# Four weight blocks split in three steps, an early half clock in the plan, and a new order table

## The chip, the cores and the metric

The kernel runs on one core of a Trainium2 chip, which has five engines that run side by side and wait for each other with semaphores: PE (matrix products), DVE and ACT (vector work), POOL (GpSimd, vector work in SBUF alone) and SP, which issues transfers. The metric is the device time of one execution in microseconds, less is better; the time before is the median of three runs.

## The reference

An attention that is causal by blocks of 64, and after it a feed-forward network with a gate made by a convolution along the sequence.

```python
scores = scale * np.matmul(q, k.transpose(0, 1, 3, 2))     # q, k, v: 8 batches, 8 heads, 576 x 64
mask = block_i >= block_j                                  # block = position // 64
attn = softmax(np.where(mask, scores, -1e9))
x = (attn @ v)                                             # heads side by side: 8 x 576 x 512
h = np.maximum(x @ w_in, 0.0)                              # w_in 512 x 1024
for k in range(3):
    conv_out += conv_w[k][None, None, :] * hp[:, k:k + S, :]
gate = 1.0 / (1.0 + np.exp(-conv_out))
return (h * gate @ w_out).astype(np.float32)               # w_out 1024 x 512
```

## The kernel before

The inputs are float32. A product that must keep float32 accuracy is made of float16 halves: an operand is split into a high half (the rounded value) and a low half (what the rounding left), and three products (high-high, low-high, high-low) are added up in PSUM. Splitting is work of the vector engines, the products are PE's.

The work goes through 8 batches. Batch 0 goes in two parts of the sequence, A (the first 256 positions) and B (the rest), with products in float32 and transposes on PE; batches 1 to 7 go whole, pair of heads by pair of heads (four pairs a batch): `stage_s` makes the scores (L1108), their maxima (L1207, DVE), the exponentials (L1210, ACT) and two float16 planes of the probabilities (L1057 to L1079, any of three engines); a DMA transposes the planes (L1097); `pair_pv` multiplies them with v (L1491) and its result is split into x (L1496, L1499, L1502). After four pairs `ffn` multiplies x with w_in (L1544), makes the gate (L1566 to L1592), splits it (L1596, L1599 the cast, L1603 the difference) and multiplies with w_out (L1637); the result is scaled (L1647, L1650) and stored.

The weights arrive once, as 16 blocks (8 of w_in, 8 of w_out) of 128 x 512 numbers. `load_w` and `decode` unpack each (L882 on ACT, L885 on POOL, L889, L892, L897 on DVE; a block's largest value L920 to L926), `scale_w` finds one scale for each matrix, and `split_w` makes the halves: `fh` multiplies a block by the scale and rounds (L951 on ACT, L954 on POOL), `fl` multiplies once more and takes the high half off (L960, DVE, `wih`/`wil` of w_in, `woh`/`wol` of w_out). The first output product (L1637) needs the halves of all eight blocks of w_out.

Order and engines come from a planner (`Plan`). Each piece of work is an operation with an engine, a planned duration and dependencies, and some can go to another engine (`other`). The table `TARGETS` has a number for each operation: a quarter of it is its place in its engine's queue, the remainder says which of the engines it takes. `Plan.order` plays the queues through with the planned durations, PE's clock among them (`speed`: full or half), and so fixes the order in which all engines get their instructions. Where it sees PE idle for over 0.4 us it puts in filling matmuls (`work`, L1774, a product of a constant with itself into a free bank), as many as fit before the next matmul by its plan.

Two operations at the very start matter here: `rounded_identity` (L643, DVE) writes `rident`, which the score products with the mask (L1337) and the transposes on PE (L1407) use; `blank` (L664) is a tile of zeros, on which the first group of fills runs. `stage_sa` makes the scores of part A (L1333, L1337), a group of eight matmuls for each pair of heads; their maxima are L1351.

## Time and profile before

| | us |
|---|---|
| median of three runs | 619.45 |
| lowest, highest | 618.64, 619.97 |
| profiled execution, its own time | 621.78 |
| its span, first to last instruction | 619.9 |
| PE, DVE, ACT, POOL busy in it | 597.5, 530.7, 481.6, 386.9 |

The profile is of one execution, whose own time is 1.88 us above its span. PE's busy time holds the filling matmuls as well. A group of matmuls is pipelined, so that the time of a group is its first start to its last end, and less than the sum of its members. The chain of waits is followed back from the last instruction: what stands on it had nothing between it and the end.

### The profile page before, as it was taken

Reading aid. Unit: us, or ns where it says so; the run is one execution under the profiler, and the core shown is the slowest. Engines: PE = TensorE matmul, PEld = TensorE weight load, DVE = VectorE, ACT = ScalarE, POOL = GpSimd, SP = SyncE. Lnnn points to the kernel's source line nnn. Section 1 sums busy time; section 2 is a strip of 40 time slices with the busy share of each in tenths; the row PEclk is TensorE's granted clock in tenths of the full one; section 3 lists DMA queues with packets and bytes.
Section 4 is the critical chain, followed back from the end, with each engine's and each line's share of the span. In section 5 each row is a group of like instructions: output and inputs, shape, how many; then the busy total and the mean of one; then the engine's idle time right before and its main releaser. Section 6 shows DMA issues by size and latency. Waiting matters only on the chain.

```text
span 619.9 us, 15505 instructions
## 1 busy us (share of the span) xinstructions
PE 597.5 (96%) x5832; PEld 381.2 (61%) x5832; DVE 530.7 (86%) x1122; ACT 481.6 (78%) x1234; POOL 386.9 (62%) x496
## 2 busy tenths in 40 slices
PE   8998899979999999999999999999999999999997
PEld 5556454447765477655775567555765667566754
DVE  5999999999889988999999998889889966973850
ACT  5999997796798659997799767978888857962721
POOL 4876665664495846986597454787786617852440
PEclk9999999999999999999999999999999999999999
DMA  8584412799938997699997699459886880594002
GB/s 296 206 293 146 139 35 92 170 224 192 255 78 217 195 221 129 139 196 218 198 189 139 143 223 227 110 116 209 188 172 117 195 145 18 108 163 120 1 1 86
DMA packets 205503, 97.77 MB, mean 158 GB/s; under 512 B 185308, under 2 KB 187636, under 8 KB 205428
## 3 DMA queue, kind: packets, MB, share of 16 engines
q1 hardware_dynamic: 203556, 93.63, 67.1%
q10 hardware_dynamic: 1872, 3.15, 1.8%
q8 instruction: 46, 0.75, 0.5%
q14 instruction: 29, 0.24, 0.1%
HBM read 41.44 MB, written 9.44 MB: 82 GB/s over the span
## 4 chain that ended last, share of the span: by engine, by line
PE 62%; DVE 25%; ACT 6%; POOL 3%; issue 2%; DMA 2%; DVEq 0%; ACTq 0%; POOLq 0%
PE banks L1637 22%; PE banks L1544 21%; PE banks L1491 8%; PE banks L1108 8%; DVE su L1207 3%; DVE t L1573 2%; PE banks L1774 2%; DVE ptbm L1063 2%; DVE t L1592 1%; DVE shared L897 1%; DVE ptbl L1063 1%; DVE st L1288 1%; DVE shared L892 1%; DVE vb L831 1%; DVE h L1063 1%
## 5 line engine op out<-in xcount | busy, mean ns | idle before, releaser
L1637 PE MATMUL banks<-woh,shared 128*128 128x512 f16 (+1 forms) x592 | 184.8, 374 | 0.3 <-DVE t L1592 0.3
L1544 PE MATMUL banks<-x,wih 128*128 128x288 f16 (+2 forms) x1024 | 156.7, 286 | 2.0 <-DVE t L1592 1.8
L1637 PEld LDWEIGHTS <-shared 128*128 128x128 f16 x888 | 82.7, 98 | 100.7 <-issue 15.0
L1544 PEld LDWEIGHTS <-wih 128*128 128x128 f16 x1024 | 98.0, 98 | 36.5 <-issue 8.6
L1207 DVE TENSOR_REDUCE su<-banks 128x1 f32<-128x192 f32 (+8 forms) x252 | 110.8, 478 | 3.1 <-PE banks L1108 2.2
L1637 PE MATMUL banks<-wol,shared 128*128 128x512 f16 (+1 forms) x296 | 110.5, 373 | 0.0
L1586 POOL TENSOR_TENSOR t<-t,shared 128x575 f32<-128x575 f32 x51 | 74.8, 1468 | 54.1 <-DVE t L1573 46.7
L1603 POOL TENSOR_TENSOR shared<-t,shared 128x576 f16<-128x576 f32 (+2 forms) x59 | 71.8, 1219 | 26.0 <-DVE shared L1599 12.8
L1544 PE MATMUL banks<-x,wil 128*128 128x288 f16 (+2 forms) x512 | 86.3, 286 | 0.6 <-DVE wil L960 0.6
L1108 PE MATMUL banks<-k,q 64*64 64x192 f32 (+9 forms) x1120 | 82.7, 414 | 3.9 <-DVE t L1592 1.1
L1491 PEld LDWEIGHTS <-vb 128*64 128x64 f16 x1848 | 63.0, 113 | 11.6 <-issue 10.9
L1573 DVE SCALAR_TENSOR_TENSOR t<-banks,cwb,t 128x575 f32<-128x575 f32 (+2 forms) x72 | 53.0, 742 | 12.5 <-ACT t L1569 7.5
L1108 PEld LDWEIGHTS banks<-k,q 64*64 64x64 f32 x1120 | 42.5, 132 | 33.9 <-issue 12.1
L1589 ACT ACTIVATE t<-t 128x576 f32<-128x576 f32 (+2 forms) x72 | 45.1, 629 | 23.1 <-POOL t L1586 16.5
L1544 PEld LDWEIGHTS <-wil 128*128 128x128 f16 x512 | 49.3, 98 | 14.9 <-DVE wil L960 1.2
L1592 DVE SCALAR_TENSOR_TENSOR t<-t,banks 128x576 f32<-128x576 f32 (+2 forms) x72 | 48.7, 680 | 8.4 <-ACT t L1589 7.6
L1569 ACT ACTIVATE t<-banks,cwb 128x576 f32<-128x576 f32 (+2 forms) x72 | 49.0, 684 | 6.6 <-DVE banks L1566 5.2
L1563 ACT ACTIVATE banks<-banks 128x576 f32<-128x576 f32 (+2 forms) x53 | 30.2, 574 | 15.8 <-PE banks L1544 15.4
L1210 ACT ACTIVATE p3f<-banks,su 128x512 f32<-128x512 f32 (+1 forms) x56 | 36.7, 659 | 5.5 <-DVE su L1207 2.2
L1582 ACT ACTIVATE shared<-banks,cwb 128x575 f32<-128x575 f32 x51 | 37.6, 738 | 1.9 <-DVE t L1573 0.8
L1647 ACT ACTIVATE stage<-banks,osc 128x512 f32<-128x512 f32 (+1 forms) x29 | 19.3, 668 | 24.7 <-PE banks L1637 24.7
L1210 ACT ACTIVATE p2f<-banks,su 128x384 f32<-128x384 f32 (+1 forms) x56 | 30.8, 552 | 8.3 <-DVE su L1207 4.4
(206 smaller groups left out, 1186.9 us busy)
## 6 DMA issues: line engine op xcount, KB each, us to landing
k<-in_k_dram SPq DMA_DIRECT2D x28, 368.0 KB, 3.7
vn<-in_v_dram SPq DMA_DIRECT2D x32, 320.0 KB, 3.9
q<-in_q_dram SPq DMA_DIRECT2D x28, 320.0 KB, 3.7
out_dram<-stage SPq DMA_DIRECT2D x24, 256.0 KB, 2.9
shared<-in_moe_w_in_dram SPq DMA_DIRECT2D x8, 512.0 KB, 4.1
shared<-in_moe_w_out_dram SPq DMA_DIRECT2D x8, 512.0 KB, 3.7
out_dram<-stage ACTq DMA_DIRECT2D x11, 256.0 KB, 3.7
k<-in_k_dram SPq DMA_DIRECT2D x4, 240.0 KB, 4.8
```

Source lines behind the costliest of these rows:

```text
L1108: nc.tensor.matmul(out[64 * y:64 * y + 64], t["q"].ap[64 * r:64 * r + 64, q0:q0 + 64], t["k"].ap[64 * r:64 * r + 64, k0:k0 + c1 - c0], sta ...
L1207: nc.vector.tensor_reduce(out=st.ap[:, k:k + 1], in_=home[hh].ap[:, x], op=ALU.max, axis=AX.X, negate=True)
L1210: nc.scalar.activation(out=y.ap[:, 0:n], in_=home[hh].ap[:, x], func=AF.Exp, bias=st.ap[:, k:k + 1], accum_out=st.ap[:, 9 + k:10 + k])
L1491: nc.tensor.matmul(y, vb.ap[:, w, c, j, :], x, start=first, stop=(z == 1 and c == jobs[-1][0]), skip_group_check=True)
L1544: nc.tensor.matmul(h(a, z), wt[:, c, fs], xs[c][xi].ap[:, x0 + a:x0 + z], start=(n + c - c0 == 0), stop=(n + c - c0 == 3 * NCC - 1))
L1569: nc.scalar.activation(out=t.ap[:, 0:no], in_=h(own, own + no), func=AF.Copy, scale=cwb.ap[:, NFC + f:NFC + f + 1])
L1573: nc.vector.scalar_tensor_tensor(out=t.ap[:, i0:no], in0=h(own + i0 - 1, own + no - 1), scalar=cwb.ap[:, f:f + 1], in1=t.ap[:, i0:no], op0 ...
L1586: nc.gpsimd.tensor_tensor(out=t.ap[:, 0:i1], in0=t.ap[:, 0:i1], in1=u.ap[:, 0:i1], op=ALU.add)
L1589: nc.scalar.activation(out=t.ap[:, 0:no], in_=t.ap[:, 0:no], func=AF.Tanh)
L1592: nc.vector.scalar_tensor_tensor(out=t.ap[:, 0:no], in0=t.ap[:, 0:no], scalar=1.0, in1=h(own, own + no), op0=ALU.add, op1=ALU.mult)
L1603: eng.tensor_tensor(out=g[1][:, f, carry:carry + no], in0=t.ap[:, 0:no], in1=g[0][:, f, carry:carry + no], op=ALU.subtract)
L1637: nc.tensor.matmul(fb.ap[:, 0:cut], g[a][:, f, cs], w[:, f, ds], start=(f == 0 and n == 0), stop=(f == NFC - 1 and n == 2))
```

## The change

It has four parts. Four of the eight blocks of w_out (9, 11, 13 and 15, `WPL`) are split in three steps: the block is multiplied by the scale in place (`sc`), copied and rounded into the high half (`h`), and the low half is the plain difference (`low`). Each step is planned on POOL and can go to another engine. The plan takes PE's clock as half until 8.5 us (`COLD`), PE as free from 1.9 us, and 0.95 us for each of the first three groups of scores. All fills use `rident`. The table has new numbers throughout.

```diff
 TARGETS = """
-0 0 4 8 16 0 4 24 28 12 16 44 64 52 129 80 196 92 185 88 181 252 140 104 280 288 448 8 12 9 4 12 16 8 40 13 32 36 20 64 44 52 44 56 96 40 200 60 60 88
+0 0 12 8 4 0 4 28 40 16 24 20 76 52 169 88 224 108 185 84 181 276 144 112 296 304 388 8 16 17 8 12 20 12 44 4 32 36 12 32 20 32 24 28 48 44 196 40 129
...
+    COLD = 8.5
+
     def order(self, targets, fill, clock):
...
-            return 1.0 if full else 2.0
+            return 1.0 if full and t > self.COLD else 2.0
...
-        free = [1.1, 0.0, 0.0, 0.0, 0.75]
+        free = [1.9, 0.0, 0.0, 0.0, 0.75]
...
+    WPL = (9, 11, 13, 15)
...
-    made = [pl.op(DVE, 2.45, rounded_identity, -80.0)]
+    made = [pl.op(DVE, 1.9, rounded_identity, -80.0)]
...
+        def sc(eng=nc.gpsimd):
+            eng.tensor_scalar(out=g.ap, in0=g.ap, scalar1=s_(), scalar2=0.0, op0=ALU.mult, op1=ALU.add)
+
+        def sc_a():
+            nc.scalar.activation(out=g.ap, in_=g.ap, func=AF.Copy, scale=s_())
+
+        def h(eng=nc.gpsimd):
+            eng.tensor_scalar(out=hi, in0=src(), scalar1=1.0, scalar2=0.0, op0=ALU.mult, op1=ALU.add)
+
+        def h_a():
+            nc.scalar.activation(out=hi, in_=src(), func=AF.Copy)
+
+        def low(eng=nc.gpsimd):
+            eng.tensor_tensor(out=lo, in0=src(), in1=hi, op=ALU.subtract)
+
+        if f in WPL:
+            o = pl.op(POOL, c_pool(512) + 0.08, sc, at, deps=[o, d], bufs=[g, fac, wm],
+                      other=((ACT, c_act(512, False, True), sc_a), (DVE, c_dve(512, True) + 0.07, partial(sc, nc.vector), True)))
+            o = pl.op(POOL, c_pool(512), h, at, deps=[o], bufs=[g],
+                      other=((ACT, c_act(512, False), h_a), (DVE, c_dve(512, True), partial(h, nc.vector), True)))
+            wdone[f] = pl.op(POOL, c_pool(512, True), low, at + 0.7, deps=[o], bufs=[g],
+                             other=((DVE, c_dve(512) + 0.01, partial(low, nc.vector), True),))
+            wsplit.append(wdone[f])
+            return
...
+        cold.append(at)
...
-            o = pl.op(PE, (0.345 + 0.06 * APM) * len(tiles), mm(tiles), at, deps=ready[0] + ready[1] + [o] + made[:2],
+            o = pl.op(PE, (0.95 if len(cold) < 4 else 0.345 + 0.06 * APM) * len(tiles), mm(tiles), at, deps=ready[0] + ready[1] + [o] + made[:2],
...
-        x = rident if len(fills) > 1 else blank
+        x = rident
```

Line numbers of the changed kernel are higher: by 3 up to the new branch, by 27 or 28 after it. The change moves instructions at many places; three follow.

The first place is PE at the start, from the end of the second group of scores (L1333 and L1337 before, L1360 and L1364 after) to the first transposes of probabilities (L1407, L1435). Before:

```order
L1337 MATMUL banks<-maskt,rident 64x64 x2
L1000 MATMUL banks<-ident,cg 128x24
L1774 MATMUL banks<-rident 128x512 x4
L1333 MATMUL banks<-k,q 128x128 x2
L1337 MATMUL banks<-maskt,rident 64x64 x2
L1333 MATMUL banks<-k,q 128x256 x2
L1337 MATMUL banks<-maskt,rident 64x64 x2
L1774 MATMUL banks<-rident 128x512 x2
L1407 MATMUL banks<-rident,p0r_84 128x128
L1407 MATMUL banks<-rident,p1r_88 128x128 x2
```

After:

```order
L1364 MATMUL banks<-maskt,rident 64x64 x2
L1360 MATMUL banks<-k,q 128x128 x2
L1364 MATMUL banks<-maskt,rident 64x64 x2
L1360 MATMUL banks<-k,q 128x256 x2
L1364 MATMUL banks<-maskt,rident 64x64 x2
L1027 MATMUL banks<-ident,cg 128x24
L1435 MATMUL banks<-rident,p0r_84 128x128
L1435 MATMUL banks<-rident,p1r_88 128x128 x2
L1299 MATMUL banks<-k,q 128x512 x2
```

The fills of four and of two are gone, and the third group of scores follows on the second. The first group of fills, ahead of these rows, has three instead of five.

At the same time on DVE, `cr` and `cg` are the convolution's weights, `shared` is a block of w_in in decode, `st` takes the maxima of the scores. Before:

```order
L643 TENSOR_SCALAR rident<-ident 128x128
L889 TENSOR_SCALAR cr<-cr 24x128
L885 TENSOR_SCALAR cg<-cg 24x128
L892 SCALAR_TENSOR_TENSOR cr<-cr 24x128
L897 SCALAR_TENSOR_TENSOR cg<-cg,cr 24x128
L1351 TENSOR_REDUCE st_117<-banks 128x1 x4
L1351 TENSOR_REDUCE st_121<-banks 128x1 x2
L889 TENSOR_SCALAR shared<-shared 128x512
```

After:

```order
L646 TENSOR_SCALAR rident<-ident 128x128
L1042 TENSOR_SCALAR q<-q 128x256
L892 TENSOR_SCALAR cr<-cr 24x128
L895 SCALAR_TENSOR_TENSOR cr<-cr 24x128
L888 TENSOR_SCALAR cg<-cg 24x128
L900 SCALAR_TENSOR_TENSOR cg<-cg,cr 24x128
L892 TENSOR_SCALAR shared<-shared 128x512
L895 SCALAR_TENSOR_TENSOR shared<-shared 128x512
L923 TENSOR_REDUCE wm<-shared 128x1
L1378 TENSOR_REDUCE st_117<-banks 128x1 x3
L900 SCALAR_TENSOR_TENSOR shared<-shared 128x512
```

Three passes of the first block's decode and its largest value (L892, L895, L923 after; L889, L892, L920 before) have moved ahead of the first maxima, and so has one scaling of q.

The second place is POOL at the split of w_out; `dg` is a diagonal for the scales, `p0f` and `ptbl` are probabilities of batch 1, L672 and L675 copy leftover columns of the gate. Before:

```order
L715 TENSOR_SCALAR dg<-ident,wm 128x128
L715 TENSOR_SCALAR dg<-ident,vs 128x128
L954 TENSOR_SCALAR woh<-shared,wm 128x512 x2
L1067 TENSOR_SCALAR p0f_81<-p0f_81,su_129 128x64
L1057 TENSOR_SCALAR ptbl<-p3f_93,su_129 128x448
L1073 TENSOR_SCALAR ptbl<-p0f_81 128x64
L672 TENSOR_SCALAR shared<-shared 128x8x127
```

After:

```order
L718 TENSOR_SCALAR dg<-ident,wm 128x128
L718 TENSOR_SCALAR dg<-ident,vs 128x128
L966 TENSOR_SCALAR shared<-shared,wm 128x512 x3
L972 TENSOR_SCALAR woh<-shared 128x512 x3
L978 TENSOR_TENSOR wol<-shared,woh 128x512 x2
L966 TENSOR_SCALAR shared<-shared,wm 128x512
L978 TENSOR_TENSOR wol<-shared,woh 128x512
L972 TENSOR_SCALAR woh<-shared 128x512
L1094 TENSOR_SCALAR p0f_81<-p0f_81,su_129 128x64
L1084 TENSOR_SCALAR ptbl<-p3f_93,su_129 128x448
L675 TENSOR_SCALAR shared<-shared 128x8x127 x2
```

Eleven passes of 512 columns stand where two stood; on DVE four subtractions of two steps in one (L960) become one plain difference (L978).

The third place is PE at the last group of fills, between the first products with w_in of batch 1 (L1544, L1572) and the products of a pair with v (L1491, L1519). Before:

```order
L1544 LDWEIGHTS wih
L1544 MATMUL banks<-x,wih 128x288
L1774 MATMUL banks<-rident 128x512 x14
L1491 LDWEIGHTS vb
L1491 MATMUL banks<-ptbh,vb 64x256
```

After:

```order
L1572 LDWEIGHTS wih
L1572 MATMUL banks<-x,wih 128x288
L1802 MATMUL banks<-rident 128x512 x3
L1519 LDWEIGHTS vb
L1519 MATMUL banks<-ptbh,vb 64x256
```

The group has 3 fills instead of 14. In the whole program 66 fills stand where 89 stood; every other matmul is still there.

## Rows read from the trace of the kernel before

**Rows 1.** The page: engine, busy us (share of the span), instructions.

```profile
PE 597.5 (96%) x5832; PEld 381.2 (61%) x5832; DVE 530.7 (86%) x1122; ACT 481.6 (78%) x1234; POOL 386.9 (62%) x496
```

**Rows 2.** Busy time by stretch, filling matmuls (L1774) alone: stretch, length, PE, PEld, clock, DMA.

```profile
0.00:40.00 40.00, 12.35 (x36) 7.62 (x36) 1.00 0.75 264
40.00:160.00 120.00, 14.96 (x53) 9.45 (x53) 0.99 0.64 159
160.00:620.00 460.00, 0.00 (x0) 0.00 (x0) 1.00 0.70 148
```

**Rows 3.** The same by stretch: PE, PEld, DVE, ACT, POOL, granted clock, DMA share, GB/s.

```profile
0.00:10.00 10.00, 8.49 (x34) 5.72 (x34) 5.02 (x27) 5.42 (x17) 3.00 (x14) 1.00 0.76 239
...
20.00:80.00 60.00, 53.19 (x416) 35.18 (x415) 59.84 (x159) 59.58 (x172) 43.77 (x62) 1.00 0.51 175
...
100.00:140.00 40.00, 35.23 (x335) 18.59 (x327) 37.98 (x98) 32.92 (x102) 24.21 (x35) 0.98 0.72 155
140.00:160.00 20.00, 20.00 (x271) 16.00 (x268) 17.34 (x38) 11.36 (x35) 9.12 (x14) 0.95 1.18 237
160.00:320.00 160.00, 156.71 (x1675) 100.98 (x1673) 148.84 (x285) 134.89 (x335) 114.30 (x137) 1.00 0.86 182
```

**Rows 4.** Chain of waits in order of time: start us, us, what, how many.

```profile
11.94 0.88 PE banks L1774 x2
...
88.11 2.19 DVE wol L960 x3
...
138.51 3.85 PE banks L1491 x66
142.36 3.40 PE banks L1774 x14
...
148.12 1.13 PE banks L1774 x4
149.24 2.24 PE banks L1491 x66
...
154.08 3.22 PE banks L1774 x14
```

**Rows 5.** Timeline 128 to 160 us: start, us, engine, line, operation; idle before in brackets.

```profile
137.09 1.42 PE L1774 MATMUL banks<-rident 128*128 128x512 f32 x5 [2.16 <-ACT p3f L1210]
...
151.52 2.14 SPq L1097 DMA_TRANSPOSE t<-h  x1
```

**Rows 6.** Timeline 0 to 16 us, PE's second fills and DVE's start.

```profile
5.88 1.35 DVE L1351 TENSOR_REDUCE st<-banks 128x1 f32<-128x256 f32 x4 [0.79 <-PE banks L1337]
...
8.01 2.08 PE L1774 MATMUL banks<-rident 128*128 128x512 f32 x4
...
8.57 0.42 DVE L889 TENSOR_SCALAR shared<-shared 128x512 uint32<-128x512 uint32 x1
...
9.18 0.66 DVE L892 SCALAR_TENSOR_TENSOR shared<-shared 128x512 int32<-128x512 int32 x1
...
9.96 0.68 DVE L920 TENSOR_REDUCE wm<-shared 128x1 f32<-128x512 f32 x1
```

**Rows 7.** Groups by line and shape: busy us, mean ns of one; idle before.

```profile
L1603 POOL TENSOR_TENSOR shared<-t,shared 128x576 f16<-128x576 f32 x45 | 59.8, 1330 | 19.0 <-DVE shared L1599 9.7 <-ACT shared L1596 7.6 <-DVE ptbm L1063 0.4
...
L960 DVE SCALAR_TENSOR_TENSOR wil<-shared,fac,wih 128x512 f16<-128x512 f32 x8 | 6.3, 810 | 0.0
...
L960 DVE SCALAR_TENSOR_TENSOR wol<-shared,wm,woh 128x512 f16<-128x512 f32 x8 | 5.9, 763 | 0.0
...
L1603 POOL TENSOR_TENSOR shared<-t,shared 128x321 f16<-128x321 f32 x6 | 5.1, 848 | 6.1 <-DVE shared L1599 3.1 <-ACT shared L1596 2.8
```

**Rows 8.** Timeline of POOL, 84 to 100 us, around the split of w_out.

```profile
84.96 1.37 POOL L954 TENSOR_SCALAR woh<-shared,wm 128x512 f16<-128x512 f32 x2
...
95.91 1.50 POOL L672 TENSOR_SCALAR shared<-shared 128x1016 f16<-128x1016 f16 x1 [6.83 <-PE banks L1637]
```

More of the change, by code (lines that the diff above doesn't have):

```diff
@@ L539, in one @@
         return pl.buf(cp, shape, dtype, tag, 1)
-    kept, gate, firstk = {}, [], []
+    kept, gate, cold = {}, [], []
     def keep(shape, dtype, tag, cap, value=0.0, at=None):
```

228 rows, old and new, of the table TARGETS are left out of this document.

## The prediction

> **What bounds the kernel now.** I read the page first: PE is busy for 597.5 us of a span of 619.9, DVE for 530.7 [rows 1]. A PE at 96% suggests a kernel that only fewer matmuls can shorten, and this change removes none that compute anything. So I asked what the 597.5 us hold. The view of the filling matmuls alone (L1774, products of constants that nobody reads) shows 27.31 us of them, all before 160 us: 12.35 in the first 40 us, 14.96 from 40 to 160, none later [rows 2]. Together with the 22.4 us in which PE stands idle (619.9 less 597.5) that is 50 us which are no work, and most of it lies in the first 160 us.
>
> The table by stretches then says who makes PE wait there. From 20 to 80 us DVE is busy for 59.84 of 60 us and ACT for 59.58, PE for 53.19 with its fills counted [rows 3]: the vector engines bound that stretch, decoding the weights and running the first softmaxes. From 160 to 320 us PE is busy for 156.71 of 160 and DVE for 148.84 [rows 3]: PE bounds it, with DVE close behind. So time is to be had before 160 us, on the path through DVE and ACT; what comes after can at most keep it.
>
> The chain of waits shows three places. Near 12 us it runs through PE and its fills (11.94, two fills, 0.88 us) [rows 4]. From there to about 136 us it runs mostly through DVE, and the eight subtractions of the split of w_out lie on it (88.11, three of them, 2.19 us) [rows 4]. From 137 to 160 us it runs through PE without a break, and in that stretch stand 5, 14, 4 and 14 fills [rows 4, 5].
>
> **The change, part by part.**
>
> *The start.* Before, PE issues four fills at 8.01 that take 2.08 us, ahead of the third group of scores, and two more at 11.94 for 0.88 us, ahead of the first turn of a score tile [rows 4, 6]. After, neither stands there: the three groups of scores follow on one another, and the number of fills up to the same place falls from 11 to 3. Up to 2.08 + 0.88 = 3.0 us leave PE's path. In exchange DVE gets the decode of the first block of w_in ahead of the first row maxima: passes of 0.42, 0.66 and 0.68 us, 1.76 us in all [rows 6]. They fall into a stretch where DVE is busy for only 5.02 of 10 us [rows 3]; the cover is the wait for PE that ends at 5.88 [rows 6]. If the block lands late, the maxima wait behind it and all 1.76 us are paid. The first fills now read the rounded identity instead of the zeros, so they wait for it; three instead of five of them leave room for that. I take the difference, 3.0 less 1.8, a gain of 1.2; bounds from a loss of 1.8 to a gain of 3.0.
>
> *The split of w_out.* Four of eight blocks are split in three steps instead of two. On DVE three of the subtractions go (2.19 / 3 = 0.73 us each on the chain, so 2.2 us) [rows 4]; the fourth stays there as a plain difference, which I put at the same price, 763 ns now [rows 7]. POOL gets four scalings and four copies and three differences, and loses two copies. A 512-column pass takes 1.37 / 2 = 0.69 us there [rows 8], so eight take 5.5. No difference of 512 columns is in the trace on POOL; 321 columns take 0.848 and 576 take 1.330 [rows 7], and in between, nearer to the wide one, 1.21, so three take 3.6. Less the 1.37 that go, POOL carries 7.7 us more. Its cover is the 6.83 us that it idles before 95.91 [rows 8]; some 0.9 us stick out, and behind them in POOL's queue are the first probabilities of batch 1, the copy of the leftover columns (L672) and the gate splits of batch 0, for which the second feed-forward product waits. Gain 2.2 less 0.9, 1.3; bounds 0 and 2.2. The rows show one thing that speaks against it: the same subtraction takes 810 ns in the split of w_in, where POOL is busy, and 763 in that of w_out, most of which runs while POOL idles [rows 7, 8]. Seven such DVE passes in this stretch would cost 7 x 0.047 = 0.3 us. The Trainium skill ("GPSIMD Engine Reference", "Key points") states a reason, that GpSimd shares its SBUF interfaces with VectorE and contends with its instructions of two SBUF inputs; by that the gain of the whole change would be 2.4 rather than the 2.7 below, and the rows, which mix both cases, can't settle it.
>
> *The late fills.* From about 125 us on, the groups of fills at the same places of PE's work go from 5, 5, 14, 4, 14 to 8, 6, 16, 0, 3. On the chain the 4 (1.13 us) go and the last 14 (3.22 us) become 3; a fill there takes 3.40 / 14 = 0.24 us, so 1.1 + 2.5 less 0.7 for the three that are added at 137 and 142 us gives 2.9 us [rows 4]. But a fill stands where a wait was planned. Where the wait is real, taking the fill away leaves idle time. The group at 154.08 begins when the last transpose that its successor needs has just been issued in full (151.52 + 2.14 = 153.66) [rows 4, 5], so a part of those 3.2 us was a true wait for the landing. DVE idles for 2.66 of the 20 us there [rows 3], so it could follow by that much at most. I take 0.7, since the gain of the first two parts reaches PE through these same waits and must not be counted twice; bounds 0 and 2.7.
>
> *The rest of the order.* The whole table was redone, and after 160 us the same number of matmuls follows. DVE has 17 instructions more in the built order and ACT 9 fewer; with three large ones gone from DVE, twenty others came to it, at its mean of 530.7 / 1122 = 0.47 us some 9 us at most, small casts and scalings being cheaper [rows 1]. From 160 to 320 us DVE has 11.2 us of idle time for its share of them [rows 3]. I charge 0.5; bounds 0 and 2.
>
> Sum: 1.2 + 1.3 + 0.7 - 0.5 = 2.7 us. The profiled execution took 621.78 us, 1.88 more than its span, and lies 2.3 above the median of the three runs, 619.45; nothing in the sum depends on that, so I take it off both: 619.1 for that execution, 616.8 for the median.
>
> **The rivals.**
>
> *Given back.* Past 160 us PE is 98% busy and DVE 93% [rows 3]. If the redone order costs its upper bound of 2 us there and POOL's excess of 0.9 lands on the path, 3.2 - 2 - 0.9 leaves 0.3, that is 619.2. For it speaks that DVE's list grew; against it that ACT, busy for 134.89 of those 160 us [rows 3], got shorter.
>
> *More comes out.* At 138.51 the 66 products of a pair took 3.85 us, at 149.24 the same took 2.24 [rows 4]; the granted clock is below 1 in these two stretches (0.98, 0.95) [rows 3], which is the lower level, 1.2 GHz, for a few microseconds, after PE had stood idle for 2.16 us [rows 5]. If PE idles less there, 1.6 us come back; with the late fills' full 2.7 the gain is 1.2 + 1.3 + 2.7 + 1.6 - 0.5 = 6.3, or 613.2. I don't put the 1.6 into the sum, since the wait in front of it is for ACT's softmax, which does not get less work there by any row.
>
> *Slower: the clock.* The fills keep PE running. In the first 40 us 36 stand before and 14 after, so at 0.24 us each PE does 5.3 us less. At 8.01 a fill still takes 2.08 / 4 = 0.52 us, twice that of 142.36 [rows 4, 6], so PE had not yet left 1.2 GHz although five fills and two groups of scores were behind it, while the clock column shows 1.00. With less work in front, the clock may rise later, or fall again between 12 and 45 us. Each fall costs what the one at 138.51 cost, 1.6 us. Two of them eat the gain; with three the time is 619.45 - 2.7 + 4.8 = 621.6. Against it: fewer planned waits mean that the real work closes up. The Trainium skill ("TensorE: Matmul & The Clock Gate", "What's actually happening") states that the half-rate state is the default and that activity releases it; by that rule the cut of fills speaks for this rival, and the trace, where PE is at half rate until past 8 us, agrees with the rule as far as it goes.
>
> **How the numbers follow.** The forecast, 615.3 to 618.2 by itself, gets 0.50: two of its terms rest on work that leaves a saturated engine and on fills that leave the path. "Given back" gets 0.23, "more" 0.12, the clock 0.15. About 0.2% either way, 1.2 us, is what a measurement of this kernel can tell from no change, so 618.2 to 620.7 counts as the same. Nearly all of the forecast and of "more" lies below 618.2: faster 0.62. "Given back" with the forecast's edge makes the same 0.22, the clock and a late landing of the first block slower 0.16. The range goes from 613.2, the rival with more, to 621.0, which takes in "given back" and the lighter half of the clock's case.
>
> **What would show it.** Right: PE's third group of scores begins before 9 us instead of after 10; the first row maxima on DVE begin within a microsecond of 5.88; POOL has no idle time of several microseconds between 85 and 96 us, and the copy L672 begins no later than 97; the product of the pair that starts at 157.30 now starts some 3 us earlier; from 160 us on PE loses no more than now. Wrong: row maxima that begin past 7.5 us behind the decode (the first term becomes a loss); a granted clock under 1 between 12 and 120 us (the clock); the same PE matmul 3 us earlier at 160 but no longer so at 320 us (given back); no fall of the clock near 138 us (more).

## The result and the profile after

The changed kernel takes 626.32 us (median of 4 runs, 624.86 to 628.80), the kernel before 619.71 in the same comparison (618.64 to 620.26): 1.0103 times the time, 95% interval 1.0076 to 1.0129. That is 6.6 us slower, where 2.7 us faster was forecast. The profiled execution took 625.77 us with a span of 623.9, 4.0 above the profiled execution of before; of the 2.6 us between that and 6.6, 2.1 come from the profiled execution of before, which lay that much above its median (621.78 against 619.71), and 0.5 from the changed kernel's, which lay below.

A lower mean clock of PE does not explain the loss. The mean granted clock of each execution is recorded: in the changed kernel's four it is 1.0, 0.999, 0.997 and 1.0, and the two at 1.0 took 625.77 and 626.86 us; the kernel before took 619.2 us on average in the 18 executions at 1.0 of all comparisons of this document, and 620.5 in the 26 at 0.997.

The page's engine row, as [rows 1] (busy us, share of the span, instructions):

```profile
PE 593.7 (95%) x5809; PEld 377.6 (61%) x5809; DVE 543.0 (87%) x1139; ACT 478.8 (77%) x1220; POOL 388.0 (62%) x495
```

PE is busy 3.8 us less and DVE 12.3 us more. The fills (L1802 now), by stretch as in [rows 2], are 66 and take 19.4 us instead of 27.3:

```profile
0.00:40.00 40.00, 4.97 (x14) 2.74 (x14) 1.00 0.81 285
40.00:160.00 120.00, 14.47 (x52) 9.22 (x52) 1.00 0.59 139
```

By stretch, as in [rows 3] (PE, PEld, DVE, ACT, POOL, clock, DMA share, GB/s):

```profile
80.00:100.00 20.00, 17.79 (x122) 10.42 (x122) 19.63 (x40) 17.59 (x43) 17.54 (x20) 1.00 0.24 67
100.00:140.00 40.00, 37.12 (x328) 19.04 (x326) 36.37 (x87) 30.50 (x91) 24.58 (x38) 1.00 0.62 141
```

From 80 to 100 us POOL is busy for 17.54 of 20 us, in the kernel before for 10.62, and PE for 17.79 instead of 18.73:

```profile
80.00:100.00 20.00, 18.73 (x135) 11.28 (x137) 18.79 (x43) 18.73 (x45) 10.62 (x14) 1.00 0.32 99
```

To see where the time went I followed PE's useful work. Every matmul that is no fill gets a fixed time by its shape, these are added up in PE's order, and the time is read at which PE starts the matmul that brings the sum to a given value (75, 100, 140, 320 and 545 us of 658). The sums are the same in all kernels, so the table shows in which stretch of work a kernel loses. Each row is one profiled execution, whose own time stands last.

| kernel | to 75 | 75 to 100 | 100 to 140 | 140 to 320 | 320 to 545 | to the end of the span | its time |
|---|---|---|---|---|---|---|---|
| before | 89.19 | 24.71 | 44.93 | 158.48 | 192.06 | 110.53 | 621.78 |
| changed | 89.32 | 28.68 | 43.35 | 157.65 | 193.41 | 111.49 | 625.77 |

All of the loss that one pair of traces shows lies between 75 and 100 (3.97 us) and behind 320 (2.31); 1.58 come back from 100 to 140 and 0.83 from 140 to 320. The 1.58 is not won by the change: in the profiled execution of before the clock fell to 1.2 GHz from 138.67 to 142.08 us, and y3 and x5 below, which have the order of before there and no fall recorded in that stretch, take 43.60 and 43.63. The first column is misleading: five other executions with the same start and order, among the experiments below, needed 86.71, 87.69, 87.74, 88.60 and 89.03 us to 75, so that before's 89.19 is the slowest of them. The changed kernel, and three more with its start and its order up to there, needed 89.32 to 89.94 (all of these are single profiled executions).

**The start.** The chain of waits of the changed kernel's first 14 us (start us, us, what):

```profile
2.13 0.36 SPq L917
...
5.38 4.37 DMA k<-in_k_dram
...
9.89 1.20 PE banks L1360 x4
```

The load of the first block of w_in (L917) is now fourth in SP's queue, where it was sixth, and the loads of k for the second and third pair of heads stand behind it. PE's third group of scores waits for the last of these until 9.89 us (it began at 10.02 before, behind the fills; in x4 below, without them, at 8.74). The first row maxima begin at 7.68 us, not at 5.88, behind the decode. The full clock is recorded from 17.24 us.

**The split of w_out.** The chain through the stretch from 95 to 113 us (as in [rows 4]):

```profile
95.20 1.10 DVE wol L963
...
98.17 0.61 DVE wol L978
...
98.82 0.39 PE banks L1665
...
100.30 1.40 POOL shared L675
...
103.27 0.81 POOL shared L1631
...
107.63 5.34 PE banks L1665 x24
```

The last half of w_out is ready at 98.78 (98.17 plus 0.61), where it was ready at 94.07 before (the last of DVE's subtractions on before's chain):

```profile
93.42 0.65 DVE wol L960
```

In the changed kernel PE's product waits for the last half, POOL's copy of the leftover columns (L675) waits for PE's product, and behind that copy in POOL's queue stand the casts, the diagonal and the differences of the gate for which ACT, DVE and then PE wait. The timeline of POOL, DVE and PE there (start, us, engine, line, operation; idle before in brackets):

```profile
84.84 2.53 POOL L966 TENSOR_SCALAR shared<-shared,wm 128x512 f32<-128x512 f32 x3
87.35 2.63 POOL L972 TENSOR_SCALAR woh<-shared 128x512 f16<-128x512 f32 x3
89.95 2.85 POOL L978 TENSOR_TENSOR wol<-shared,woh 128x512 f16<-128x512 f32 x2
...
94.01 1.74 POOL L978 TENSOR_TENSOR wol<-shared,woh 128x512 f16<-128x512 f32 x1
```

```profile
87.89 1.03 DVE L963 SCALAR_TENSOR_TENSOR wol<-shared,wm,woh 128x512 f16<-128x512 f32 x1
...
90.00 1.79 DVE L834 SCALAR_TENSOR_TENSOR vb<-vn,vs,vb 128x640 f16<-128x640 f32 x1
...
95.12 1.18 DVE L963 SCALAR_TENSOR_TENSOR wol<-shared,wm,woh 128x512 f16<-128x512 f32 x1
```

```profile
98.82 0.38 PE L1665 MATMUL banks<-wol,shared 128*128 128x512 f16 x1 [1.56 <-DVE wol L978]
...
107.63 0.38 PE L1665 MATMUL banks<-woh,shared 128*128 128x512 f16 x1 [1.78 <-DVE t L1620]
```

POOL works without a pause from 84.84 to 96.77, 11.9 us for its eleven passes. On DVE a subtraction of 512 columns, 0.74 us in the quiet, takes up to 1.03 beside POOL's copies and 1.18 beside a difference, and a split of v (L834), 0.87 in the quiet, takes 1.79 beside a difference; another split of v (93.87 us) takes its 0.87 there. PE stands idle for 1.56 and 1.78 us and runs seven fills where three were.

The chain from 86 to 98.78 us is DVE's own list; POOL's last rounding had ended at 96.78. From the first of its subtractions to the last half DVE needs 12.7 us, where it needed 7.7. Of these 5.0 us, the subtractions that left give back 2.1; passes that run beside POOL are longer by about 3.0 in sum; and about 4.1 are other work that the new order puts ahead of the last half (a third split of v, a maximum of v, five passes of the gate's convolution and some small scalings), which stood elsewhere before. The passes by form (busy us, mean ns of one):

```profile
L978 POOL TENSOR_TENSOR wol<-shared,woh 128x512 f16<-128x512 f32 x3 | 4.6, 1542 | 0.0
...
L963 DVE SCALAR_TENSOR_TENSOR wol<-shared,wm,woh 128x512 f16<-128x512 f32 x4 | 3.9, 970 | 0.1
...
L966 POOL TENSOR_SCALAR shared<-shared,wm 128x512 f32<-128x512 f32 x4 | 3.8, 958 | 0.1
...
L972 POOL TENSOR_SCALAR woh<-shared 128x512 f16<-128x512 f32 x4 | 3.7, 936 | 0.0
```

### The profile page after: what moved, and what is told of

It reads as the page before. It is cut to its first block, busy times and chain, and to the rows that moved or that the text cites. A ratio compares the mean times of both kernels' runs of the same rounds, so it can differ in the third digit from the quotient of the medians.

```text
span 623.9 us, 15508 instructions
## 1 busy us (share of the span) xinstructions
PE 593.7 (95%) x5809; PEld 377.6 (61%) x5809; DVE 543.0 (87%) x1139; ACT 478.8 (77%) x1220; POOL 388.0 (62%) x495
## 4 chain that ended last, share of the span: by engine, by line
PE 45%; DVE 30%; ACT 11%; POOL 5%; issue 4%; DMA 3%; SPq 1%; DVEq 0%; POOLq 0%; ACTq 0%
PE banks L1665 16%; PE banks L1572 16%; PE banks L1519 6%; DVE su L1234 6%; PE banks L1135 5%; DVE ptbm L1090 3%; DVE t L1620 2%; DVE t L1601 2%; DVE ptbl L1090 2%; DVE h L1090 2%; DVE vb L834 1%; POOL shared L1631 1%; DMA k<-in_k_dram 1%; POOL t L1614 1%; DVE x L1530 1%
## 5 line engine op out<-in xcount | busy, mean ns | idle before, releaser
L1572 PE MATMUL banks<-x,wih 128*128 128x288 f16 (+2 forms) x1024 | 157.1, 286 | 6.7 <-DVE t L1620 2.4
L1572 PEld LDWEIGHTS <-wih 128*128 128x128 f16 x1024 | 98.6, 98 | 41.8 <-issue 12.8
L1234 DVE TENSOR_REDUCE su<-banks 128x1 f32<-128x128 f32 (+8 forms) x252 | 110.7, 478 | 5.1 <-PE banks L1135 4.3
L1572 PE MATMUL banks<-x,wil 128*128 128x288 f16 (+2 forms) x512 | 86.0, 286 | 0.0
L1135 PE MATMUL banks<-k,q 64*64 64x256 f32 (+9 forms) x1120 | 82.5, 414 | 2.3 <-DVE t L1620 1.1
L1601 DVE SCALAR_TENSOR_TENSOR t<-banks,cwb,t 128x575 f32<-128x575 f32 (+2 forms) x72 | 53.5, 744 | 19.5 <-ACT t L1597 12.7
L1519 PEld LDWEIGHTS <-vb 128*64 128x64 f16 x1848 | 61.6, 111 | 10.2 <-issue 9.4
L1135 PEld LDWEIGHTS banks<-k,q 64*64 64x64 f32 x1120 | 43.0, 132 | 32.2 <-issue 12.3
L1572 PEld LDWEIGHTS <-wil 128*128 128x128 f16 x512 | 49.6, 98 | 14.1 <-issue 0.7
L1237 ACT ACTIVATE p1f<-banks,su 128x192 f32<-128x192 f32 (+1 forms) x56 | 24.9, 445 | 12.5 <-DVE su L1234 9.2
```

Of the source, the lines that this page charges most:

```text
L1135: nc.tensor.matmul(out[64 * y:64 * y + 64], t["q"].ap[64 * r:64 * r + 64, q0:q0 + 64], t["k"].ap[64 * r:64 * r + 64, k0:k0 + c1 - c0], sta ...
L1234: nc.vector.tensor_reduce(out=st.ap[:, k:k + 1], in_=home[hh].ap[:, x], op=ALU.max, axis=AX.X, negate=True)
L1237: nc.scalar.activation(out=y.ap[:, 0:n], in_=home[hh].ap[:, x], func=AF.Exp, bias=st.ap[:, k:k + 1], accum_out=st.ap[:, 9 + k:10 + k])
L1519: nc.tensor.matmul(y, vb.ap[:, w, c, j, :], x, start=first, stop=(z == 1 and c == jobs[-1][0]), skip_group_check=True)
L1572: nc.tensor.matmul(h(a, z), wt[:, c, fs], xs[c][xi].ap[:, x0 + a:x0 + z], start=(n + c - c0 == 0), stop=(n + c - c0 == 3 * NCC - 1))
L1601: nc.vector.scalar_tensor_tensor(out=t.ap[:, i0:no], in0=h(own + i0 - 1, own + no - 1), scalar=cwb.ap[:, f:f + 1], in1=t.ap[:, i0:no], op0 ...
```

## The experiments

Of each, the ratio is to the kernel before on the same chip. Where an order is mixed from two kernels, the operations that the plan of before starts ahead of a given time keep one kernel's sequence on every engine and the others follow in the sequence of the other; the plan then also chooses fills and PSUM banks anew. The columns of the table above follow for each after its reading (to 75; 75 to 100; 100 to 140).

### The split, undone and done alone

```diff
-    WPL = (9, 11, 13, 15)
+    WPL = ()
```

> The changed kernel with the old split of all eight blocks of w_out (four roundings on POOL, four on ACT, eight subtractions in a row on DVE), every other operation in its changed place. Theory A (the three-step split makes the halves of w_out late, by 98.77 instead of 94.07 us, and the 4.8 us that PE is behind at 118 us come from there): the last half of w_out ends before 95 us, PE reaches the same work at 118 us within 1.5 us of before, and the time falls from 626.3 to 621 to 623. Rival B (the loss is the new order of the other work, on PE and DVE): the time stays at 625 to 627, whatever the split takes.

Measured: 628.12 us, 1.0128 (1.0094 to 1.0162). It was meant to give the split back and was slower than the changed kernel; neither theory had that. To 75, 89.94; then 29.17; then 46.57. Eight subtractions in a row hold the splits of v, the gate's work and ACT behind them: PE waits 2.56 us for DVE's part of the gate (L1649) at 100.70, although all halves are there by 93. The edit took the split away and put a worse order in its place, so that it says nothing on the split.

The kernel before with the new branch and its places alone:

```diff
+    WPL = (9, 11, 13, 15)
...
+        if f in WPL:
+            o = pl.op(POOL, c_pool(512) + 0.08, sc, at, deps=[o, d], bufs=[g, fac, wm],
...
```

> The kernel before, its order unchanged but for the split of w_out: blocks 9, 11, 13 and 15 in three steps as in the change, eleven passes in a row on POOL, one plain difference on DVE, the rounding of block 10 on ACT. Theory A (the split costs 4 to 5 us): the last half of w_out ends past 97 us and the time is 623 to 626. Rival B (the new order costs it): 619 to 621. My prediction put the split at a gain of 1.3 (bounds 0 and 2.2): 617.5 to 619.7.

Measured: 625.21 us, 1.0094 (1.0060 to 1.0128): theory A. To 75, 86.71; then 28.71, 4.0 more than before; then 45.00, as before. POOL, DVE and PE in this stretch:

```profile
82.48 2.03 POOL L993 TENSOR_SCALAR shared<-shared,wm 128x512 f32<-128x512 f32 x3
84.60 3.00 POOL L999 TENSOR_SCALAR woh<-shared 128x512 f16<-128x512 f32 x3
87.56 3.41 POOL L1005 TENSOR_TENSOR wol<-shared,woh 128x512 f16<-128x512 f32 x2
...
93.24 0.61 POOL L999 TENSOR_SCALAR woh<-shared 128x512 f16<-128x512 f32 x1
```

```profile
88.25 1.71 DVE L861 SCALAR_TENSOR_TENSOR vb<-vn,vs,vb 128x640 f16<-128x640 f32 x1
...
93.89 0.69 DVE L1005 TENSOR_TENSOR wol<-shared,woh 128x512 f16<-128x512 f32 x1 [2.21 <-POOL woh L999]
```

```profile
91.02 0.41 PE L1691 MATMUL banks<-wol,shared 128*128 128x512 f16 x1 [2.61 <-POOL wol L1005]
```

POOL needs 11.4 us for the eleven passes, PE waits 2.61 us for a difference on POOL, and DVE waits 2.21 us for the last rounding on POOL. In the old order, then, the split by itself costs 5.8 us by the ratio. Some of it may be the clock's: the four executions have a mean granted clock of 0.995, 0.997, 0.988 and 0.991, and the first two took 624.07 and 623.95 us, 3.5 more than the kernel before at 0.997.

### What a pass on POOL costs DVE

The kernel before with passes on POOL whose output nobody reads, put where POOL is idle (from 89 to 96 us by the trace of before); the second kernel has ten `tensor_scalar` instead:

```diff
+    def extra():
+        nc.gpsimd.tensor_tensor(out=probe, in0=blank.bitcast(F32).unsqueeze(1).broadcast_to([P, 2, P]), in1=wih[:, 0, 0:256].rearrange("p (c n) -> p c n", n=P), op=ALU.subtract)
...
+    for _ in range(6):
+        pl.op(POOL, 0.71, extra, 0.0).port = False
```

> The kernel before, and six more passes on POOL that subtract one SBUF tile of 256 columns from another into a scratch tile nobody reads, put into the stretch from 89 to 96 us where POOL is idle. Theory G (a POOL pass with two SBUF inputs slows the DVE passes beside it): the subtractions L960 and L831 on DVE that run beside it take 0.2 to 0.9 us longer each, in sum 1.5 to 2.5 us from 88 to 96 us (0.44 us in 86 to 100 before), PE is 1 to 2 us later at 100 us, time 621 to 622. My prediction's row: 0.05 us for each pass, time within 0.5 us of before.

> The same as with two inputs, but ten passes on POOL with one SBUF input (a scaling of 256 columns) in the same stretch, about as long in sum. Theory G: a pass with one input leaves DVE alone: the DVE passes beside it keep 0.72 to 0.75 and 0.87 us, time 619.5 to 620.5. Rival H (any POOL work slows DVE): lengthening and time as with two inputs.

Measured: two inputs 623.42 us, 1.0075 (1.0045 to 1.0105); one input 621.73 us, 1.0028 (1.0016 to 1.0040). From 75 to 100: 27.95 and 25.81, against 24.71. POOL and DVE with two inputs, then with one, and the quiet value from the kernel before:

```profile
87.61 6.78 POOL L1811 TENSOR_TENSOR probe<-blank,wih 128x256 f16<-128x256 f32 x6
```

```profile
89.21 1.28 DVE L860 SCALAR_TENSOR_TENSOR vb<-vn,vs,vb 128x640 f16<-128x640 f32 x1
...
90.48 1.09 DVE L989 SCALAR_TENSOR_TENSOR wol<-shared,wm,woh 128x512 f16<-128x512 f32 x1
91.50 1.29 DVE L860 SCALAR_TENSOR_TENSOR vb<-vn,vs,vb 128x640 f16<-128x640 f32 x1
...
93.78 0.63 DVE L824 TENSOR_SCALAR osc<-fac,vs 128x2 f32<-128x2 f32 x1
```

```profile
87.56 8.07 POOL L1811 TENSOR_SCALAR probe<-blank 128x256 f16<-128x256 f32 x10
```

```profile
88.87 1.01 DVE L860 SCALAR_TENSOR_TENSOR vb<-vn,vs,vb 128x640 f16<-128x640 f32 x1
...
91.54 0.88 DVE L989 SCALAR_TENSOR_TENSOR wol<-shared,wm,woh 128x512 f16<-128x512 f32 x1
```

```profile
90.22 0.87 DVE L831 SCALAR_TENSOR_TENSOR vb<-vn,vs,vb 128x640 f16<-128x640 f32 x1
...
91.08 0.74 DVE L960 SCALAR_TENSOR_TENSOR wol<-shared,wm,woh 128x512 f16<-128x512 f32 x1
```

Beside a POOL pass with two inputs each of these DVE passes is 0.35 to 0.42 us longer (0.74 to 1.09, 0.87 to 1.28 and 1.29), a scaling of two columns too (0.21 to 0.63). Beside one with one input the two shown are 0.14 longer (0.88, 1.01), another 0.07. Theory G was right on two inputs, with a time above its 621 to 622; on one input it was wrong, and rival H in part: such a pass of 256 columns costs DVE a third as much or less. By their ratios the two kernels cost 4.7 and 1.7 us. With two inputs POOL is done 1.85 us before its next work, so that all of it came through DVE; with one input POOL is busy up to its next copy, which may have part in the 1.7. POOL's idle time was not free while DVE was the bound.

The plain differences of blocks 11, 9 and 13 in the changed kernel moved to DVE, by their three numbers in the table (all numbers times 20, to have room):

```diff
-7520 7600 7760
+17765 17925 18085
```

(A remainder of 1 picks DVE; their places are behind its operations at 888, 896 and 904 of the changed table.)

> The changed kernel with all four plain differences of the split of w_out on DVE instead of one, so that POOL has no pass with two SBUF inputs between 84 and 96 us. Theory G (these passes slow DVE and hold POOL): DVE's passes L963 and L834 come down to 0.74 and 0.87 us (1.18 and 1.79 at most in the changed kernel), 3.3 us of lengthening in 86 to 100 us become about 1.3, and three passes of 0.68 come to DVE; the time 624.5 to 626. Rival J (DVE is the bound there, what counts is the number of its passes): 627 to 628.5.

Measured: 629.08 us, 1.0158 (1.0141 to 1.0175), rival J. The lengthening of DVE's passes from 86 to 100 us (each pass less the quarter quantile of its form in the kernel before, added up) falls from 3.31 to 1.78 us, but three passes more on DVE outweigh it: 75 to 100 takes 30.31. Most of what is left of the lengthening stands beside POOL's copies and scalings, passes with one input, most of them of 512 columns:

```profile
87.73 2.68 POOL L1001 TENSOR_SCALAR woh<-shared 128x512 f16<-128x512 f32 x3
```

```profile
88.28 1.03 DVE L992 SCALAR_TENSOR_TENSOR wol<-shared,wm,woh 128x512 f16<-128x512 f32 x1
...
91.74 1.28 DVE L863 SCALAR_TENSOR_TENSOR vb<-vn,vs,vb 128x640 f16<-128x640 f32 x1
```

They are 0.29 and 0.41 us above the quiet values, so the small price of one input in y4 does not carry over to the copies and scalings of this change.

### The start

The kernel before without the fills of four and two (in `work`):

```diff
         fills.append(k)
+        k = 0 if len(fills) in (2, 3,) else k
```

> The kernel before without the fills of four at 8.01 us and of two at 11.94 us, all else in place. My prediction's first term: their 3.0 us leave the path, 616.5 to 618.5. Theory A: the third group of scores waits for the transfer of k, which lands near 9.7 us, and from 14 us on DVE bounds the kernel; PE's third group begins within 0.4 us of before, and the time is 619 to 620.5. Rival C (the clock): PE stays at 1.2 GHz for longer, later stages are slower, over 621.

Measured: 620.67 us, 1.0000 (0.9981 to 1.0019): theory A by the ratio, my first term refuted. PE waits for POOL's scaling of q, which waits for its transfer, and starts no sooner than with the fills; the second row is the execution of x2, where they run:

```profile
8.74 0.80 PE L1333 MATMUL banks<-k,q 64*128 64x128 f32 x4 [1.92 <-POOL q L1015]
```

```profile
6.76 1.23 PE L1828 MATMUL banks<-rident 128*128 128x512 f32 x4
8.72 0.49 PE L1387 MATMUL banks<-k,q 64*128 64x128 f32 x4 [0.72 <-POOL q L1069]
```

In x2 the four fills took 1.23 us and not the 2.08 of [rows 6], and the group behind them began at 8.72 and not at 10.02: the profiled execution of before was one in which PE came to 2.4 GHz late.

The changed start on the kernel before (first 14 us, with its fills), and the old start on the changed kernel (first 12 us):

```diff
 TARGETS (operations that the plan of before starts ahead of 14 us: the changed numbers)
...
-    COLD = 8.5
+    COLD = -1.0
-        free = [1.9, 0.0, 0.0, 0.0, 0.75]
+        free = [1.1, 0.0, 0.0, 0.0, 0.75]
```

(The four lines of code are the second kernel's; the first keeps 8.5 and 1.9.)

> The other way round: the kernel before with the first 14 us in the changed order, with the changed fills and plan of the start, then its own order and its own split. Theory E: 622 to 622.8, PE's second and third groups of scores at 7 and 9.8 us behind the transfers of k, full clock only past 15 us. My prediction's first term, taken alone: 618 to 619. Rival I: 619.5 to 620.5.

> The changed kernel with the first 12 us back in the order of before (transfers of q and k ahead of the blocks of w_in, the first row maxima ahead of the decode) and with the old rule for fills (11 ahead of the first turns of a score tile); from there the changed order and the new split of w_out. Theory E (the start costs the changed kernel 2.2 to 2.4 us of its 6.6): 623.5 to 624.5, PE 2 us earlier than in the changed kernel from 20 to 80 us, full clock before 13 us. Rival I (what is won at the start is waited for later, since DVE bounds the stretch behind it): 626 to 627.

Measured: the changed start alone costs the kernel before 3.1 us (622.71, 1.0050, 1.0035 to 1.0065), theory E; to 75 it takes 91.45 us, and the second group of scores begins at 7.70 us, later still than in the changed kernel (6.98), where it was 5.94. The row puts that wait down to a pass over the block of w_in on POOL:

```profile
7.70 0.80 PE L1360 MATMUL banks<-k,q 64*128 64x128 f32 x4 [1.72 <-POOL shared L888]
```

The chain of its start runs through the load of that block, its decode on DVE, the row maxima behind it and ACT to the third group of scores:

```profile
2.14 3.66 DMA shared<-in_moe_w_in_dram
...
7.75 0.61 DVE st L1378 x2
...
9.81 1.34 PE banks L1360 x4
```

The full clock comes late as well: it is recorded from 17.16 to 18.77 us on in the six profiled kernels with the changed start and its fills (the changed one, x1, x3, w2, y2, z2), and from 4.39 to 12.38 in the six executions with the start and the fills of before. So the loads of k, the decode ahead of the maxima and the late clock all come with this start, and z2 does not separate them.

Taking it out of the changed kernel gave 626.43 us, 1.0102 (1.0083 to 1.0120), so no time; yet in its profiled execution (624.15 us, the fastest of its four) PE is 1.7 us earlier at 75 (87.62) and still at the end of the span. Rival I has the times and theory E the trace; this stays open.

The changed kernel with more fills at the start, the late groups held at its numbers:

```diff
-        x = rident
+        k = {16: 8, 17: 6, 18: 16, 19: 0, 20: 0, 21: 3}.get(len(fills) + 1, k)
+        x = rident if len(fills) > 1 else blank
...
-    COLD = 8.5
+    COLD = -1.0
```

> The changed kernel with the old rule for the fills of the start (no planned half clock, PE free from 1.1 us, first five fills on the zeros): 5, 9, 5 and 2 fills stand ahead of and between its first score groups, where 3 stand in all; the fills after 70 us are those of the changed kernel. Theory C (in the changed kernel PE stays at 1.2 GHz until 17.24 us because it has too little to do, and that costs part of the 2.4 us it is late at the start): full clock from before 10 us, first turns of a score tile before 12 us, time 624 to 625.5. Theory D (the start waits for its transfers, since a block of w_in is loaded ahead of q and k): the clock may rise earlier, PE's third group of scores begins at 9.8 us all the same, time 626 to 627.

Measured: 633.02 us, 1.0214 (1.0195 to 1.0232). To 75 it is 1.3 us faster than the changed kernel (88.05, outside the 89.32 to 89.94 of the four with the changed start), with the transfers as they are and although its third group of scores begins later, at 10.51: full clock is recorded from 5.16 us, in the changed kernel from 17.24 and in the profiled execution of before from 12.38. So the fills seem to bring something there, by one execution; then it takes 27.63, and 52.00 from 100 to 140, 8.7 us more, with waits for ACT. The plan chooses PSUM banks by its own times, so this kernel differs from the changed one in more than its fills, and I did not find out which of it costs the 8.7 us.

The first 74 us of the changed kernel ahead of the order of before:

```diff
 TARGETS (operations that the plan of before starts ahead of 74 us: the changed sequence; the rest: that of before)
```

> The first 74 us in the changed order, with the changed plan of the start and its fills, then the order of before, with the old split of w_out in its old places; fills after 74 us by the plan's rule. Theory E (the start and the order up to 80 us cost some 2.4 us, the split the rest): 622 to 623.5, PE 2 us or more behind a usual execution of before at 70 us. My prediction's first term: a gain of 1.2, 618 to 619. Rival F (all of the loss is the split): 619.5 to 620.5.

Measured: 626.32 us, 1.0108 (1.0091 to 1.0126), more than any theory had, with the old split; to 75, 91.28. But the seam falls into the stretch where all engines are full, ahead of the point at which 75 is reached, so that its loss can't be told from the seam's, and z2 is the better cut.

### The fills

The kernel before without its last two groups, and without any:

```diff
         fills.append(k)
+        k = 0 if len(fills) in (16, 17,) else k
```

> The kernel before without its last two groups of fills (four at 148.12, fourteen at 154.08 us), all else in place. My prediction's third term took 0.7 us for them, bounds 0 and 2.7: 617.3 to 620. Theory A (they stand in real waits for the transposes): 619.5 to 620.5, and the product of the pair at 157.3 begins within 0.5 us of before. Rival C: a fall of the clock behind 148 us, 621 or more.

> The kernel before without any of its 89 fills, all else in place: 27.31 us of PE's work less. If fills lay on the path (the third term of my prediction and part of the first), 3 us or more are gained: under 617. Theory A (they stand in real waits): 619 to 621. Rival C (they keep the clock up): the granted clock falls below 1 in several places before 160 us, and each fall costs about 1.6 us: over 622.

Measured: 619.45 us, 0.9987 (0.9969 to 1.0005) without the last eighteen; 622.21 us, 1.0035 (1.0018 to 1.0052) without all 89. The late fills stood for the most part in true waits (theory A): in the profiled execution without them PE idles 1.57 and 1.20 us where the last fourteen were, for POOL (L1073) and for the transposes of h. A gain as small as my 0.7 lies within the interval. All 89 are worth 2.2 us, not a cost (rival C): without them the granted clock falls again and again near the start (windows as in [rows 3]):

```profile
8.00:12.00 4.00, 3.00 (x21) 1.88 (x21) 3.68 (x12) 2.17 (x7) 3.37 (x8) 0.82 1.01 374
...
20.00:24.00 4.00, 4.00 (x25) 2.44 (x23) 3.81 (x9) 4.00 (x14) 3.92 (x7) 0.60 0.04 11
```

### The order of the rest

The old split with the four subtractions spread among the splits of v, and the same with the old start:

```diff
 TARGETS (the four subtractions that come back to DVE: places among the splits of v)
...
-    WPL = (9, 11, 13, 15)
+    WPL = ()
```

> The changed kernel with the old split as in x1, but with the four subtractions that come back to DVE spread among its other work (between the splits of v, as in the kernel before) and not eight in a row. Theory A (the three-step split costs the changed kernel some 3 to 5 us; x1 was slow because eight subtractions in a row held the work behind them): 622 to 624. Rival B (the order of the rest costs it whatever the split): 626 or more.

> The same, and the first 12 us back in the order of before with the old fill rule there: what is left of the change is the order from 12 us on and the later fills. My prediction's fourth term: a loss of 0.5, bounds 0 and 2, with the late fills' 0.7 as a gain: 619 to 621.5. Theory E and A together (start 3, split 3 to 5): 620 to 621. Rival B: 624 or more.

Measured: 625.58 us, 1.0110 (1.0059 to 1.0162) and 624.20 us, 1.0070 (1.0043 to 1.0098). The first lies between its theories, the second with rival B: with split and start both undone, 4.2 us are left. From 75 to 100 they take 27.51 and 26.56: the order without the split loses 1.8 us and more there. In w2 the last half of w_out still ends at 97.05 us, with the old split of all eight blocks, since the same other work stands ahead of it on DVE:

```profile
95.65 1.40 DVE L992 SCALAR_TENSOR_TENSOR wol<-shared,wm,woh 128x512 f16<-128x512 f32 x2
```

So the new order, with the start and the split of before, was cut in two, from 160 us on and from 12 to 160 us:

```diff
 TARGETS (operations that the plan of before starts behind 160 us, then from 12 to 160 us: the changed sequence; the rest: that of before)
```

> The kernel before up to 160 us, and the changed order of all engines from there to the end; old split, old start, old fills. My prediction's fourth term: a loss of 0.5, bounds 0 and 2: 619.7 to 621.7. Theory K (from the traces: the changed kernel loses 1.4 us between 320 and 510 us of PE's work and 0.9 in its last 100 us): 621 to 622.5. If it is below 619, this order is a gain to carry over.

> The other half of what was left in w3 (624.2): the changed order from 12 to 160 us with the later fills, old split, old start, and the order of before from 160 us on. Theory K (w3's loss is behind 160 us): 620 to 621.5. Rival B (it is the order of 12 to 160 us): 622.5 to 624.

Measured: the order from 160 us on, 620.09 us, 0.9999 (0.9982 to 1.0017); the order from 12 to 160 us, 621.83 us, 1.0041 (1.0011 to 1.0070). In its trace the late order gains 1.4 us from 140 to 320 and loses 2.2 behind 320, as in the changed kernel, but in the time nothing is left of that; theory K was wrong. The middle order takes 26.56 from 75 to 100, 1.8 more, and costs 2.5 us by its ratio, with an interval from 0.7 to 4.3; the median lies between the two theories, nearer to K, the ratio nearer to rival B. Two of its eight executions, at a mean granted clock of 0.992, took 624.85 and 626.55 us and the other six 620.25 to 622.93, so how much of the 2.5 is the clock's is open.

## Why the prediction was wrong

**What bounds the kernel: right.** The vector engines bound the first 100 us, and most of the loss came from there. But I drew from it that work taken off DVE is a gain, and did not ask what the replacement does to DVE.

**The start: wrong in sign.** I took 1.2 as a gain, with a bound of -1.8; alone it costs 3.1 us (z2). The step that failed is "four fills leave PE's path". They stood in the wait for q (x4), and the 0.52 us of one fill came from an execution with a late clock. With no gain to set against it, what the change puts ahead of the scores remains as a loss. I had priced its decode ahead of the maxima, and named row maxima that begin past 7.5 us as the sign of a loss; they began at 7.68, and in z2 the chain runs through that decode. What I did not cost is the move on SP's queue, a block of w_in ahead of the loads of k, which gave the wait from 5.38 to 9.75 us on the changed kernel's chain. How the 3.1 us divide among these and the late clock stays open.

**The split: wrong in sign, and the largest error.** I took a gain of 1.3 with bounds 0 and 2.2; alone it costs 3.5 to 6 us (x2). The gain itself was as I took it: the subtractions that left give DVE 2.1 us. Three other terms failed. POOL's eleven passes were to take 9.1 us (7.7 more than 1.37) and took 11.9: a scaling or copy 0.95 us and not 0.69, a difference 1.54 and not 1.21. DVE's passes beside them were to be 0.3 us longer in all; from 86 to 100 us the lengthening is 3.31 us, 0.44 before. And what sticks out of POOL's idle time was put at 0.9 us of delay, where the last half of w_out came 4.7 us late, with PE, POOL and ACT in a chain behind it. In x2 it is late through POOL, for which DVE waits 2.21 us; in the changed kernel through DVE's list, with its longer passes and the work that the order puts ahead. The row of 810 against 763 ns was the hint; I used the mean of a form over quiet and loaded passes as the price of the load, which y3 shows at 0.4 us for a single pass.

The Trainium skill ("GPSIMD Engine Reference", "Key points") says that GpSimd shares SBUF interfaces with VectorE and contends with its instructions of two SBUF inputs. I gave it 0.3 us in a sentence beside the sum; y3 bears it out with numbers. The Trainium skill ("SBUF — State Buffer", "SBUF: two separate sides") calls the shared pair of ports an exclusive lock: the instruction that starts first has it, and "the other fully blocks". The rows here neither show nor refute that: the lengthening of single passes was 0.35 to 0.42 us in y3 and from nothing to 0.92 in the changed kernel, beside POOL passes whose own time may hold waiting too (1.06 us on average for 256 columns in y3, where one of 321 columns took 0.848 on average before [rows 7]).

**The late fills: right that they are true waits.** 0.7 was taken from bounds of 0 and 2.7; the run gives 0.8 with an interval that holds 0 and leaves out 2.7 (x5).

**The rest of the order: too small.** 0.5 was charged, for the stretch behind 160 us. There it costs nothing that the time shows (v1); from 12 to 160 us it costs 2.5 us by the ratio (v2), for which my sum had no term; in the changed kernel and in w2 it shows as other work ahead of the last half of w_out on DVE. The counts of instructions by engine, from which I argued, don't show it.

**The rivals.** "Slower" was the right side, and its time of 621.6 was exceeded. It had the clock rise later, and that is what every profiled execution of the changed start with its fills shows (17.16 to 18.77 us, against 4.39 to 12.38 with the start of before); but its price stood for two or three falls between 12 and 120 us, and no such fall is recorded in the changed kernel. The 1.6 us of "more comes out" are a matter of the execution and not of the change: the clock did not fall near 138 us in the profiled execution of the changed kernel, nor in some of the order of before. The rival that I lacked is that POOL's idle time is not free.

**The sum.** Alone, split, start and middle order cost 5.8, 3.1 and 2.5 us (the ratios less 1, times 620), 11.4 in all; together 6.4. They do not add up. A reason may be that they meet in the same waits from 75 to 100, which is argued and not shown; taking the split or the start out of the changed kernel gave nothing in the time (w2, z1), both together 2 us (w3). How the 6.4 divide among them in the changed order is not settled.

## What to carry to other kernels

Idle time of GpSimd is no free room while VectorE is the bound: price each pass moved there by what it does to the VectorE passes beside it, from rows that ran beside such a pass, and let the last step that a matmul waits for not be the last in its queue. Look at what a new order puts ahead of the last piece that the bound engine owes to the others, and not only at the pieces that leave. A filling matmul on the chain tells nothing before the wait under it is known; leave it out in a run first. And look at the loads that a moved operation drags along in the issuing queue.

## What the hardware showed

VectorE's passes grew by 0.35 to 0.42 us beside GpSimd passes with two SBUF inputs of 256 columns, and by 0.07 to 0.14 beside those with one (y3, y4), but by 0.29 and 0.41 beside POOL's copies and scalings, most of them of 512 columns (x3); a scaling of two columns grew from 0.21 to 0.63 (y3). GpSimd's own pass of 512 columns went from 0.69 to 0.95 us in the changed kernel. One and the same start runs differently in each execution: six profiled executions that have the start of before reached the same matmul (75 us of work) between 86.71 and 89.19 us, with full clock recorded from 4.39 to 12.38 us on. And 89 fills of 27.3 us, left out, made the kernel 2.2 us slower.
